# Exchanging the partition halves of odd heads' tokens in a DeltaNet and Fourier-mixing kernel, with other queues for the first loads

## The chip, the core and the metric

The kernel runs on one core of a Trainium2 chip. The metric is the device time of one execution in microseconds (us). The profile is of one execution; its times are counted from the start of the span, in us unless ns is written.

## The reference

Two blocks run one after the other on float32 data. The first is a delta-rule recurrence over 768 tokens for 4 batches and 8 heads of 48 numbers:

```python
def _attn_ref(q, k, v, beta):                       # q, k, v: (4, 8, 768, 48)
    k_n = k / (np.linalg.norm(k, axis=-1, keepdims=True) + 1e-06)
    state = zeros((B, H, D, D))
    for t in range(S):
        kt, vt, bt = k_n[:, :, t], v[:, :, t], beta[:, :, t, None]
        y[:, :, t] = einsum('bhd,bhde->bhe', q[:, :, t], state)
        v_old = einsum('bhde,bhd->bhe', state, kt)
        state = state + bt[..., None] * einsum('bhd,bhe->bhde', kt, vt - v_old)
```

The second takes the result as x of shape (4, 768, 384):

```python
    mixed = np.real(fft(fft(x, axis=1), axis=2))
    u = x + mixed
    un = (u - mean(u)) / sqrt(var(u) + 1e-06)       # over the last axis
    return u + maximum(un @ w_ch1, 0) @ w_ch2       # w_ch1: 384 x 1536, w_ch2: 1536 x 384
```

The two weight matrices come as float64 and are turned into float32 on the chip.

## The kernel before

Tokens are worked on in units: unit u is 128 tokens of one batch with all 8 heads, so there are 4 x 6 = 24 units. Within a unit the recurrence is written for two chunks of 64 tokens. A chunk's own triangular system is inverted, so that its new values are a matrix times v less a matrix times the state; then the state is advanced. One chunk is one step of the recurrence, 12 steps per batch, each of which needs the state left by the one before.

A head is 2j + s, with j from 0 to 3 (NJ) and s 0 or 1; s = 1 are the odd heads. Token c*64 + t of a unit lies in partition c*64 + t, so chunk c is partition half c, for every head. Most matmuls of the recurrence use 64 x 64 corners of TensorE's 128 x 128 array: the row half is the partition half of the operands, the column half is the partition half of the output. `mm` (line 477) and `tr` (line 480) issue all of these matmuls, so their instructions have these two lines, and `copy` (lines 486, 488 and 490) nearly all of the evictions from PSUM.

What the program does, in its own terms:

- Units 0 to 5 (batch 0) are rounds 0 (four units) and 1 (two units). Their keys are loaded first (`load`, line 583), turned (`turn`, line 604), multiplied with themselves (`keys`, line 628), and inverted on VectorE (`begin16` line 777, `invert16` line 838). `queries` (line 1902) then loads q and v. `join` (line 885) and `blocks` (line 953) make the chunk's inverse; its masked copies are ScalarE's.
- Batch 0 then runs `ready`, `values0` (line 1064), `chain0` (line 1081) and `outputs0` (line 1138) per unit. `chain0` accumulates the new values in PSUM (`z.bU`), copies them to u (line 1123), multiplies them with the keys into a state that stays in PSUM (`bS`), and copies that (line 1135). Two odd/even pairs of 64 partitions are copied, one instruction per s.
- Batches 1 to 3 come in rounds of three units: `prepare` (line 1911) and `consume` (line 1925), which calls `blocks`, `ahead` (line 1009), `step` (line 1160) twice and `outputs` (line 1226). In `step`, line 1190 subtracts the state's part from u, line 1219 adds to the state, and in `outputs`, line 1254 adds into x. Lines 1190 and 1254 run once per s on 64 partitions, because the values of chunk c lie in one partition half.
- When a batch's recurrence is complete, `mixing` (line 1869) does the Fourier transforms, the normalisation and the two layers of the MLP. Their matmuls use all 128 rows.

Two matmuls stand for others: line 2036 (early) and line 2043 write PSUM that nobody reads. They are put in by `idle` (line 2029) where TensorE would have nothing.

**What sets the order.** Nothing is issued as it is written. Each piece of work is registered with `P.op` (line 60): the engines that may do it with an estimated cost, what it reads and writes, a priority, and a due time. `Plan.schedule` (line 158) then plays the program through in a model with these costs, the DMA's landing times (eight DMAs in flight, line 279), the clock of TensorE and the fetching of its instructions, and `issue` (line 329) writes the instructions of every engine in the order found. Each engine executes its list in that order. Constants at lines 30 to 46, 529, 1829 and 2000 to 2001 set priorities, hold-backs and due times: `IV` and `IV1` (line 1829) are what rounds 0 and 1 get for the early inversion, `MD` (line 529) is the spacing of the due times of batch 0's units, `E0, E1, D1` (line 2001) bound the stretch in which stand-in matmuls may be put in freely.

**Loads.** All loads but two are issued by SyncE (SP) at line 525. A load of a unit's q, k or v is one DMA of 128 partitions x 8 heads x 192 bytes; for units 6 to 13 it is two, of 121 and 7 partitions (`ROW`, line 585). `bt` (beta) and `pack` (identity and masks) are issued by ScalarE. `f_b` (line 1851) turns beta by six small matmuls and `g_b` (line 1860) copies it to `bcol`.

Of the kernel before, what the change touches and what calls it, by code (L numbers as in the profile page):

```python
# [32 lines left out]
LOOK, HOLD, EARLY = 1e9, 0.2, 25.7  # L33
# [3 lines left out]
LATE = 0.0  # L37
# [8 lines left out]
TARGET, SPANW = 692.9, 2.6  # L46


class Plan:
# [108 lines left out]
    def schedule(self, pick, limits, switch, idle=None, span=()):  # L158
# [27 lines left out]
        self.bursts = []  # L186
        done, n, now = 0, len(ops), 0.0
        order, strict, last = [], True, None
        while done < n:
            progressed = False  # L190
            for e in self.ENG:
# [74 lines left out]
                dur = o.engs[e]  # L266
                if e == "PE":
# [111 lines left out]
def kernel(  # L379
# [24 lines left out]
    GS = 6  # L404
# [137 lines left out]
    def unit(u):  # L542
# [10 lines left out]
        z.K = v(512, 512, "p (h t) -> p h t", h=H)  # L553
        z.V = v(1024, DM, "p (h t) -> p h t", h=H)
# [14 lines left out]
        z.Q = z.LT  # L569
# [8 lines left out]
        z.U = z.ut.rearrange("p (h d) -> p h d", h=H)  # L578
# [4 lines left out]
    def load(z, what):  # L583
        pr = 0
        for x0, x1 in ((0, ROW), (ROW, 128)) if 6 <= z.u < 14 else ((0, 128),):
            rows = slice(z.T * 128 + x0, z.T * 128 + x1)
            kb = 200 * (x1 - x0) / 128
            if "k" in what:
                dma(z.K[x0:x1, :, 0:D], k[z.b, :, rows, :].rearrange("h p d -> p h d"),
                    [z.aK(x0, x1)], pr, kb=kb)  # L590
            if "q" in what:
                dma(z.Q[x0:x1, :, 0:D], q[z.b, :, rows, :].rearrange("h p d -> p h d"),
                    [z.aLT(x0, x1)], pr, kb=kb)
            if "v" in what:
                dma(z.V[x0:x1], v[z.b, :, rows, :].rearrange("h p d -> p h d"), [z.aV(x0, x1)], pr,
                    [units[GS - 1].aK()] if z.u < GS else [], kb=kb)
# [7 lines left out]
    def turn(z, pr, what=(1, 0), after=()):  # L604
# [3 lines left out]
        def fn(e):  # L608
            for i, a in enumerate(what):
                w = (z.Q, z.K)[a].rearrange("p (j s) t -> p j (s t)", s=2)  # L610
# [56 lines left out]
    def gram(z, ro, ul, pr):  # L667
# [4 lines left out]
        def fn(e):  # L672
            for j in range(NJ):
                for s, c in ((0, 0), (1, 1), (0, 1), (1, 0)):
# [3 lines left out]
                       z.QK[pr_, 0:n, c, j, :], j == 0)  # L678
# [33 lines left out]
    def scale_v(z, ro, ul, pr):  # L712
        def fn(e):
            I(eng(e).tensor_tensor(  # L714
                z.V, z.V, ro.nr(160 + 8 * ul, 8)[:, :, None].broadcast_to([128, H, D]),
                op=ALU.mult))
        vec(DM, fn, [ro.anr(160, 32)], [z.aV()], pr)
# [167 lines left out]
    def join(z, ul, ro, pr):  # L885
# [17 lines left out]
        for a in range(2):  # L903
            P.op({"ACT": t_act(256) + 0.08}, lambda e, a=a: copy(e, F[:, :, a], Du, (m0, m1)[a]),
# [12 lines left out]
        for a in range(2):  # L917
            P.op({"ACT": t_act(256) + 0.08}, lambda e, a=a: copy(e, F[:, :, a], E, (m0, m1)[a]),
# [90 lines left out]
    def ahead(z, pr):  # L1009
# [3 lines left out]
        def f1(e):  # L1013
            for j in range(NJ):
                for s, c in ((0, 0), (1, 1), (1, 0), (0, 1)):
                    a = slice(64 * c, 64 * c + 64)
                    mm(psum(b1[c])[64 * s:64 * s + 64, 64 * j:64 * j + 64], z.K[a, 2 * j + s, :],
                       z.TT[a, 2 * j + s, :], j == 0)

        def f2(e):  # L1020
            for j in range(NJ):
                for s, c in ((0, 0), (1, 1), (1, 0), (0, 1)):
                    a, x = slice(64 * c, 64 * c + 64), 64 * (c ^ s)
                    mm(psum(b2[s])[x:x + 64, D * j:D * j + D], z.TT[a, 2 * j + s, :],
                       z.V[a, 2 * j + s, :], j == 0)
# [7 lines left out]
        us = z.ut.rearrange("p (j s d) -> p s j d", s=2, d=D)  # L1033
        W = DM // 2

        def g2(e):
            copy(e, us[:, 0], psum(b2[0])[:, 0:W].rearrange("p (j d) -> p j d", d=D))
        P.op(either(W, 0.1), g2, [], [A(z.ut, 0, DM, 0, 1), A(z.ut, 0, DM, 64, 65)], pr - EV,
             use=[b2[0]], lat=LA)
        for c in range(2):  # L1040
            def g3(e, c=c):
                a, x = slice(64 * c, 64 * c + 64), slice(64 - 64 * c, 128 - 64 * c)
                copy(e, us[a, 1], psum(b2[1])[x, 0:W].rearrange("p (j d) -> p j d", d=D))
# [116 lines left out]
    def step(z, c, pr):  # L1160
# [8 lines left out]
        for i in range(k):  # L1169
# [34 lines left out]
            if n == 2 * NT - 1:  # L1204
                continue
# [875 lines left out]
```

## Time and profile before

| | us |
|---|---|
| median of three runs | 671.3 |
| the three runs | 664.39, 671.3, 673.06 |
| the profiled execution | 667.22 |
| its span | 665.4 |
| TensorE busy (PE) | 650.6 |
| VectorE busy (DVE) | 504.1 |
| ScalarE busy (ACT) | 270.3 |
| GpSimd busy (POOL) | 36.3 |
| mean clock granted to TensorE | 0.997 of full speed |

PE is a matmul, PEld a weight load, which may overlap with matmuls. Each matmul of this kernel is two records in the profile, so 16 matmuls are x32. A matmul's shape is written rows*columns of the stationary operand, then the output's shape. In a group's line the numbers after the bar are its busy time in us, the mean duration of one in ns, and the idle time before it with what ended it. In a table by stretches, the columns behind the length are the engines' busy times, then the granted clock, the share of time for which the 16 DMA engines were busy, and GB/s.

### The profile page before, as it was taken

What the parts mean: (1) busy time and instruction counts of PE and PEld (TensorE: products, weight loads), DVE (VectorE), ACT (ScalarE), POOL (GpSimd) and SP (SyncE); (2) the same over time, 40 slices, a digit from 0 to 9 for tenths busy, and PEclk for the clock granted to TensorE, in tenths of its full rate; (3) what the DMA queues carried; (4) which work ended last, traced back from release to release, by engine and by line L of the source; (5) the groups of instructions that cost most, each with busy time, mean ns of one, the idle gap of its engine ahead of it and who ended that gap; (6) DMA issues with size and microseconds to landing.
All of it is one profiled execution on the core that took longest, in us unless ns stands there. A gap on an engine that the chain in (4) does not pass through costs nothing.

```text
span 665.4 us, 23378 instructions
## 1 busy us (share of the span) xinstructions
PE 650.6 (98%) x10184; PEld 535.8 (81%) x10184; DVE 504.1 (76%) x1479; ACT 270.3 (41%) x758; POOL 36.3 (5%) x34
## 2 busy tenths in 40 slices
PE   8998899999899999999999999999999999999998
PEld 7888888777678777877777778777777789999997
DVE  3998589999964399999922589998981865877473
ACT  5579787621354332524333433244324313321220
POOL 3004223130000000000000000000000000000000
PEclk9999899999999999999999999999999999999999
DMA  9905565100033113001212120000000000000000
GB/s 201 304 33 105 146 142 148 35 0 25 1 63 75 38 26 73 1 1 26 63 38 50 50 49 2 24 2 3 26 2 3 26 3 0 25 1 25 1 25 25
DMA packets 82667, 31.38 MB, mean 47 GB/s; under 512 B 75651, under 2 KB 79716, under 8 KB 82436
## 3 DMA queue, kind: packets, MB, share of 16 engines
q1 hardware_dynamic: 82372, 29.65, 18.0%
q8 instruction: 80, 1.31, 0.8%
q10 hardware_dynamic: 192, 0.23, 0.1%
q14 instruction: 23, 0.19, 0.1%
HBM read 25.16 MB, written 4.72 MB: 45 GB/s over the span
## 4 chain that ended last, share of the span: by engine, by line
PE 80%; DVE 13%; ACT 3%; issue 2%; DMA 1%; DVEq 0%; SPq 0%; ACTq 0%
PE pp L477 75%; PE pp L480 3%; DVE rr L938 2%; DVE tmp L933 2%; ACT us L486 1%; PE pp L2043 1%; PE pp L2036 1%; DMA x<-in_moe_w_ch_dram 1%; DVE rr L795 1%; DMA us<-in_q_dram 1%; DVE tmp L855 1%; DVE w L861 1%; DVE us L714 0%; ACT w L1795 0%; DVE us L696 0%
## 5 line engine op out<-in xcount | busy, mean ns | idle before, releaser
L477 PE MATMUL pp<-R,w 128*128 128x256 f32 (+1 forms) x832 | 184.1, 368 | 0.6 <-ACT R L486 0.6
L477 PEld LDWEIGHTS pp<-R,w 128*128 128x128 f32 x832 | 145.1, 190 | 19.7 <-ACT R L486 0.7
L477 PE MATMUL pp<-w,R 128*128 128x384 f32 x384 | 135.1, 495 | 0.0
L477 PEld LDWEIGHTS pp<-w,R 128*128 128x128 f32 x384 | 70.0, 190 | 41.0 <-issue 0.2
L486 ACT ACTIVATE us<-pp 128x256 f32<-128x256 f32 (+3 forms) x186 | 65.0, 388 | 61.6 <-PE pp L477 48.3
L1475 ACT ACTIVATE R<-pp 128x512 f32<-128x512 f32 x48 | 28.7, 597 | 106.8 <-PE pp L477 106.8
L477 PE MATMUL pp<-us 64*64 64x48 f32 (+3 forms) x2496 | 61.7, 235 | 1.6 <-issue 1.3
L938 DVE TENSOR_TENSOR rr<-rr,tmp 128x108 f32<-128x108 f32 (+13 forms) x180 | 57.6, 330 | 2.3
L477 PEld LDWEIGHTS pp<-us 64*64 64x64 f32 (+1 forms) x2496 | 52.3, 136 | 8.7 <-issue 5.5
L933 DVE TENSOR_TENSOR tmp<-rr 128x210 f32<-128x210 f32 (+12 forms) x180 | 57.3, 328 | 2.1
L1190 DVE TENSOR_TENSOR u<-u,pp 64x192 f32<-64x192 f32 x66 | 22.4, 351 | 39.3 <-PE pp L477 37.7
L477 PEld LDWEIGHTS pp<-u,us 64*64 64x64 f32 x1472 | 39.7, 134 | 14.7 <-issue 10.5
L477 PE MATMUL pp<-u,us 64*64 64x48 f32 x1472 | 45.7, 221 | 2.8 <-issue 1.3
L486 ACT ACTIVATE x<-pp 64x192 f32<-64x192 f32 (+1 forms) x81 | 25.2, 324 | 54.2 <-PE pp L477 50.1
L1254 DVE TENSOR_TENSOR x<-x,pp 64x192 f32<-64x192 f32 x66 | 23.2, 351 | 24.5 <-PE pp L477 23.3
L486 ACT ACTIVATE R<-pp 128x192 f32<-128x192 f32 (+7 forms) x80 | 22.5, 333 | 43.0 <-PE pp L477 21.8
L1650 DVE TENSOR_TENSOR us<-us,pp 128x256 f32<-128x256 f32 x64 | 26.7, 418 | 12.5 <-ACT us L486 10.3
L477 PE MATMUL pp<-tab,R 128*96 128x193 f32 (+2 forms) x192 | 33.0, 328 | 0.1
L477 PEld LDWEIGHTS pp<-st,us 48*64 48x64 f32 x1232 | 22.6, 134 | 12.3 <-issue 9.8
L477 PEld LDWEIGHTS pp<-tab,R 128*96 128x96 f32 (+2 forms) x192 | 30.8, 163 | 1.4 <-DVE R L1279 0.6
L2043 PE MATMUL pp<-pack 64*64 64x256 f32 (+1 forms) x206 | 31.1, 384 | 0.0
L486 ACT ACTIVATE u<-pp 64x192 f32<-64x192 f32 (+1 forms) x68 | 22.2, 326 | 17.0 <-PE pp L477 11.7
(165 smaller groups left out, 978.1 us busy)
## 6 DMA issues: line engine op xcount, KB each, us to landing
out_dram<-x SPq DMA_DIRECT2D x11, 384.0 KB
us<-in_k_dram SPq DMA_DIRECT2D x16, 192.0 KB
us<-in_q_dram SPq DMA_DIRECT2D x16, 192.0 KB
us<-in_v_dram SPq DMA_DIRECT2D x16, 192.0 KB
us<-in_v_dram SPq DMA_DIRECT2D x8, 181.5 KB
ws<-in_moe_w_ch_dram SPq DMA_DIRECT2D x3, 484.0 KB
us<-in_k_dram SPq DMA_DIRECT2D x8, 181.5 KB
us<-in_q_dram SPq DMA_DIRECT2D x8, 181.5 KB
```

Source lines behind the costliest of these rows:

```text
L477: I(nc.tensor.matmul(o, lhsT=lhsT, rhs=rhs, start=start, stop=stop, skip_group_check=True))
L480: I(nc.tensor.matmul(o, lhsT=src, rhs=ident[p0:p0 + n, p0:p0 + n], is_transpose=True, start=start, stop=True, skip_group_check=True))
L486: I(nc.scalar.activation(o, i, ACT.Copy, **({} if scale is None else {"scale": scale})))
L795: vec(1760, lambda e: I(nc.vector.transpose(R, ro.gd(0, 4).rearrange("p (n c) -> p c n", c=32))), [ro.agd(0, 4)], [aR], pr)
L855: I(eng(e).tensor_tensor(T_, sub(j + 1, 16, j, j + 1).broadcast_to([128, 2, n, j]), sub(j, j + 1, 0, j).broadcast_to([128, 2, n, j]), op=A ...
L933: I(eng(e).tensor_tensor(T_, R[:, :, j + 1:32, j:j + 1].broadcast_to([128, ns, n, j]), R[:, :, j:j + 1, 0:j].broadcast_to([128, ns, n, j]) ...
L938: I(eng(e).tensor_tensor(R[:, :, j + 1:32, 0:j], R[:, :, j + 1:32, 0:j], T_, op=ALU.add))
L1190: I(nc.vector.tensor_tensor(U[:, s], U[:, s], psum(b1[s])[a, s0:s1].rearrange("p (j d) -> p j d", d=D), op=ALU.subtract))
L1254: I(nc.vector.tensor_tensor(w, w, v, op=ALU.add))
L1475: I(nc.scalar.activation(o, s, ACT.Relu))
L1650: vec(256, lambda e: I(nc.vector.tensor_tensor(o, i0(), i1(), op=ALU.add)), [], [aH] + list(wr), pr - EV, use=n)
L2043: I(nc.tensor.matmul(pst[two[0]][x, 0:256], lhsT=w[x, 0:n], rhs=w[x, 0:256], start=True, stop=True, skip_group_check=True))
```

## The change

For odd heads, k and v (and q from unit 6 on) are loaded with their partition halves exchanged: tokens 64 to 127 into partitions 0 to 63 and the reverse. Chunk c of head 2j + s is then partition half c ^ s. The new values of one chunk fill all 128 partitions, even heads in one half and odd heads in the other, and u is stored chunk by chunk (c, j, d). The row and column halves of the matmuls, their banks and the copies follow from that. Beta is needed in both arrangements. A load is three DMAs: the even heads, and the odd heads in two halves; for units 0 to 5, keys and values may go to SP or to ScalarE, and the queries are loaded as before the exchange in one DMA. `SPLIT` no longer cuts `step` (it was 1 there). Many constants of the planner are different, some estimated costs too, so all engines' lists are made anew. The core of the diff:

```diff
-LOOK, HOLD, EARLY = 1e9, 0.2, 25.7
+LOOK, HOLD, EARLY = 1e9, 0.181, 25.7
-GAP2 = 0.304
-PLOOK, PHOLD, PEND = 23.4, 0.367, 116.9
+GAP2 = 0.885
+PLOOK, PHOLD, PEND = 15.4, 0.154, 91.9
-FORCE = 540.9
-BLOCK, LEAD, SEEK, LAND, HOLDUP = 256, 60, 1.0, 2.4, 0.0
+FORCE = 548.4
+BLOCK, LEAD, SEEK, LAND, HOLDUP = 256, 60, 1.0, 2.4, 0.4
+CHARGE = 0.9
-TARGET, SPANW = 692.9, 2.6
+TARGET, SPANW = 709.5, 2.6
...
+                if e == "POOL" and o.port:
+                    self.lock = now + 0.2
+                if e == "DVE" and not o.banks and self.lock < now < free["POOL"]:
+                    self.lock, dur = 1e9, dur + CHARGE
...
     def dma(o, i, wr, pr, rd=(), kb=200, q="SP"):
-            I((nc.sync if q == "SP" else nc.scalar).dma_start(out=o, in_=i))
-        P.op({q: 0.45}, fn, rd, wr, pr, lat=2.0, kb=kb)
-    M0, MP, MX, MN, MA, MT, MD = 91.8, 128.0, 19.9, 38, 17.7, 5.85, 4.52
+            I(eng(e).dma_start(out=o, in_=i))
+        t = 0.45 if kb > 100 else 0.6
+        P.op({"SP": t, "ACT": 0.46} if q == "ANY" else {q: t}, fn, rd, wr, pr, lat=2.0, kb=kb)
+    M0, MP, MX, MN, MA, MT, MD = 99.6, 128.0, 22, 39.1, 12.7, 5.85, 6.22
...
     def load(z, what):
-        for x0, x1 in ((0, ROW), (ROW, 128)) if 6 <= z.u < 14 else ((0, 128),):
...
+            if y == "q" and z.u < GS:
+                dma(t[:, :, :, 0:D].rearrange("p s j d -> p j s d"),
+                    w[z.b, :, r0:r0 + 128, :].rearrange("h p d -> p h d"), [wr()], pr, rd)
+                continue
+            for s, x0, x1, o in ((0, 0, 128, 0), (1, 0, 64, 64), (1, 64, 128, -64)):
+                dma(t[x0:x1, s, :, 0:D],
+                    w[z.b, s:H:2, r0 + x0 + o:r0 + x1 + o, :].rearrange("h p d -> p h d"),
+                    [...], pr, rd, kb=100 * (x1 - x0) / 128,
+                    q="ANY" if z.u < GS else "SP")
...
     def ahead(z, pr):          # the evictions of the values
-            copy(e, us[:, 0], psum(b2[0])[:, 0:W]...)            # 128 partitions
-        for c in range(2):
-                copy(e, us[a, 1], psum(b2[1])[x, 0:W]...)        # 64 partitions
+        for s in range(2):
+            for c in range(2):
+                    a, x = slice(64 * c, 64 * c + 64), 64 * (c ^ s)
+                    copy(e, z.ut[a, W * (c ^ s):W * (c ^ s) + W], psum(b2[s])[x:x + 64, 0:W])
...
     def values0(z, pr):
-                        a, y = slice(64 * c, 64 * c + 64), 64 * (c ^ s)
-                        mm(psum(z.bU[s])[y:y + 64, D * j:D * j + D], z.TT[a, 2 * j + s, :], z.V[a, 2 * j + s, :], j == 0)
+                        a = slice(64 * (c ^ s), 64 * (c ^ s) + 64)
+                        mm(psum(z.bU[c])[a, D * j:D * j + D], z.TT[a, 2 * j + s, :], z.V[a, s, j, :], j == 0)
...
     def chain0(z, c, pr, part=(0, 1)):
-        for s in range(2):
-                copy(e, z.ut.rearrange("p (j s d) -> p s j d", s=2, d=D)[a, s],
-                     psum(z.bU[s])[y:y + 64, 0:W].rearrange("p (j d) -> p j d", d=D))
+        P.op(either(W, 0.02), lambda e: copy(e, z.ut[:, W * c:W * c + W], psum(z.bU[c])[:, 0:W]),
+             [], aU, pr - EV - 5, use=[z.bU[c]], lat=LA)
...
     def outputs0(z, pr):
-                        a = slice(64 * c, 64 * c + 64)
-                        mm(psum(z.bO[s])[a, ...], z.LT[a, 2 * j + s, :], z.U[a, 2 * j + s, :], ...)
+                        a = slice(64 * (c ^ s), 64 * (c ^ s) + 64)
+                        mm(psum(z.bO[s])[64 * c:64 * c + 64, ...], z.LT[a, 2 * j + s, :], z.U[a, c, j, :], ...)
...
     def step(z, c, pr):
-                            for q, y in ((1, 64 * c), (0, 64 - 64 * c)):
-                                mm(psum(b1[s])[y:y + 64, D * j:D * j + D], z.QK[r, q, c, j, :], so[r, D * j:D * j + D], j == js[0])
+                        for q, y in ((1, half_(s)), (0, half_(1 - s))):
+                            mm(psum(b1[1 - q])[y, D * j:D * j + D], z.QK[r, q, c ^ s, j, :], so[r, D * j:D * j + D], j == 0)
-                [z.aQT(), z.aE(1, c), A(so, s0, s1)]
+                [z.aQT(), z.aE(1, 0), z.aE(1, 1), A(so, 0, W)]
-                for s in range(2):
-                        I(nc.vector.tensor_tensor(U[:, s], U[:, s], psum(b1[s])[a, s0:s1]..., op=ALU.subtract))
+                I(nc.vector.tensor_tensor(U, U, psum(b1[0])[:, 0:W], op=ALU.subtract))
-                        mm(t[64 * s:64 * s + 64, ...], z.K[a, 2 * j + s, :], z.U[a, 2 * j + s, :], j == js[0])
+                    mm(t[64 * s:64 * s + 64, ...], z.K[half_(s), s, j, :], z.U[half_(s), c, j, :], j == 0)
...
     def outputs(z, pr):
-                    a, y = slice(64 * c, 64 * c + 64), 64 * (c ^ s)
-                    mm(psum(b[c])[y:y + 64, ...], z.LT[a, h, :], z.U[a, h, :], j == 0)
+                    a = slice(64 * (c ^ s), 64 * (c ^ s) + 64)
+                    mm(psum(b[s])[64 * c:64 * c + 64, ...], z.LT[a, h, :], z.U[a, c, j, :], j == 0)
-        for c in range(2):
-            for s in range(2):
+        for s in range(2):
+            for cs in ((0,), (1,)) if z.T == 0 else ((0, 1),):
...
-    NW, IV, IV1, WP = 8, 18.9, 9.07, -14.4
+    NW, IV, IV1, WP = 8, 7.32, 9.07, -8.86
...
+        for T in range(NT):        # in f_b: beta with its halves exchanged
+            for c in range(2):
+                x = 128 * T + 64 - 64 * c
+                mm(t[64 * c:64 * c + 64, ...], bt[:, x:x + 64], ident[0:B * H, 0:B * H], False)
...
-    WAIT, GATHER, URGENT, FIRST = 6.3, 1.59, 8.45, 15
-    E0, E1, D1 = 1.0, 10.0, 125.6
+    WAIT, GATHER, URGENT, FIRST = 14.4, 1.47, 9.13, 14.2
+    F0, F1 = 255.0, 275.0
+    E0, E1, D1 = 0.502, 10.0, 117.8
...
-    P.schedule(pick, LIM, SW, idle, ((E0, D1),))
+    P.schedule(pick, LIM, SW, idle, ((E0, D1), (F0, F1)))
```

Where a line of the diff was long, "..." stands for the part that both sides share.

More of the change, by code (lines that the diff above doesn't have):

```diff
@@ new lines, in step, with f2, g2 @@
+        if n == 2 * NT - 1:
+            return
+        b2 = Bank("attn")
+        def f2(e):
+            t = psum(b2)
+            for j in range(NJ):
+                for s in range(2):
+                    mm(t[64 * s:64 * s + 64, D * j:D * j + D], z.K[half_(s), s, j, :],
+                       z.U[half_(s), c, j, :], j == 0)
+        def g2(e):
+            if n == 0:
+                copy(e, sn[:, 0:W], psum(b2)[:, 0:W])
+            else:
+                I(nc.vector.tensor_tensor(sn[:, 0:W], so[:, 0:W], psum(b2)[:, 0:W], op=ALU.add))
@@ L1226, in outputs @@
+        P.op({"PE": 0.4}, f2, [z.aK(), aU], [], pr, "64", new=b2, lat=LE, col=144, ni=32)
+        vec(W + 30, g2, [A(so, 0, W)] if n else [], [A(sn, 0, W)], pr - EV - 5, use=[b2])
     def outputs(z, pr):
```

212 lines of the change are left out of this document (86 added, 126 removed).

## The prediction

> **What bounds the kernel now.** I read the totals first, then busy time by stretch, then TensorE's stand-in matmuls (lines 2036 and 2043, whose products nobody reads) in the same stretches, then the timeline of one step of the recurrence of batch 0, then the groups that the edit touches.
>
> ```profile
> span 665.4 us, 23378 instructions
> PE 650.6 (98%) x10184; PEld 535.8 (81%) x10184; DVE 504.1 (76%) x1479; ACT 270.3 (41%) x758; POOL 36.3 (5%) x34
> ```
>
> TensorE is busy for 98% of the span. The question is how much of that is work. The stretches, all instructions (columns: length, then PE, PEld, DVE, ACT, POOL busy):
>
> ```profile
> 0.00:40.00 40.00, 36.77 (x744) 32.09 (x744) 29.19 (x116) 21.97 (x62) 5.78 (x10) 1.00 0.83 220
> 40.00:100.00 60.00, 55.37 (x1940) 50.21 (x1936) 47.69 (x110) 51.75 (x142) 16.89 (x14) 0.97 0.49 112
> 100.00:187.00 87.00, 84.38 (x851) 64.40 (x850) 84.88 (x245) 36.54 (x104) 12.73 (x8) 1.00 0.15 40
> 187.00:665.40 478.40, 474.12 (x6662) 389.07 (x6662) 342.36 (x1011) 160.01 (x453) 0.94 (x3) 1.00 0.11 26
> ```
>
> and line 2043 alone (PE, PEld):
>
> ```profile
> 0.00:40.00 40.00, 19.39 (x152) 14.11 (x152) 1.00 0.83 220
> 40.00:100.00 60.00, 6.70 (x38) 2.57 (x38) 0.97 0.49 112
> 187.00:665.40 478.40, 4.34 (x14) 2.23 (x14) 1.00 0.11 26
> ```
>
> So after 187 us TensorE is idle for 478.40 - 474.12 = 4.3 us and in stand-ins for 4.3: 470 of 478 us are work, and nothing that shortens another engine there is worth more than those 8.6 us. Before 40 us it is the other way round: 3.2 idle, 19.4 in line 2043 and 5.4 in line 2036. From 40 to 100 it idles 4.6 and stands in for 6.7. Time can be won only where TensorE does no work, and nearly all of that lies before 100 us.
>
> The recurrence of batch 0, its first part, on ScalarE and then on TensorE:
>
> ```profile
> 48.77 0.66 ACT L486 ACTIVATE u<-pp 64x192 f32<-64x192 f32 x2
> ...
> 51.96 0.67 ACT L486 ACTIVATE u<-pp 64x192 f32<-64x192 f32 x2
> ```
>
> ```profile
> 51.99 0.67 PE L477 MATMUL pp<-us 64*64 64x48 f32 x29
> 52.59 0.50 PE L477 MATMUL pp<-us,pb 64*32 64x32 f32 x18
> 53.79 0.43 PE L477 MATMUL pp<-us,pb 64*32 64x32 f32 x14 [0.70 <-issue]
> 54.15 0.49 PE L477 MATMUL pp<-u,us 64*64 64x48 f32 x10
> ...
> 57.36 1.50 PE L477 MATMUL pp<-u,us 64*64 64x48 f32 x45
> ```
>
> Two u copies run one after the other on ScalarE before the state's matmuls (54.15) may start; TensorE serves other units meanwhile. "issue" is a stop with nothing to wait for in the record.
>
> The groups that shrink:
>
> ```profile
> L1254 DVE TENSOR_TENSOR x<-x,pp 64x192 f32<-64x192 f32 x66 | 23.2, 351 | 24.5 <-PE pp L477 23.3 <-ACT pb L486 0.2
> L1190 DVE TENSOR_TENSOR u<-u,pp 64x192 f32<-64x192 f32 x66 | 22.4, 351 | 39.3 <-PE pp L477 37.7 <-ACT x L486 0.4
> L486 ACT ACTIVATE u<-pp 64x192 f32<-64x192 f32 x47 | 15.2, 324 | 2.3 <-PE pp L477 0.8 <-DVE u L488 0.5
> L1219 DVE TENSOR_TENSOR st<-st,pp 128x192 f32<-128x192 f32 x30 | 10.5, 350 | 12.4 <-PE pp L477 12.0
> ```
>
> 192 columns cost 350 ns on 64 partitions (line 1190) and on 128 (line 1219): joining two halves saves a whole instruction.
>
> **The change part by part**, against the profiled execution: 667.22 us, a span of 665.4 and 1.8 around it. The three runs took 664.39, 671.3 and 673.06; it lies 0.6% below their median.
>
> *Tiles of TensorE.* Each matmul is two records; in starts of the trace, a group that uses all four 64x64 corners starts a matmul every 29 ns (the step's first group, 32 records, from 339.43 to 339.93: 0.50 us), one that uses two corners every 58 ns (the step's second group, 16 records at 343.30 in about 0.46). The change permutes corners. In `step` the first group keeps four and the second two; `ahead` keeps its corners; `outputs` keeps four. In batch 0, `values0` falls from four to two: 0.60 us (51.99 to 52.59) to 0.93. `outputs0` rises from two to four: the 45 records at 57.36 are it and a state group, 1.29 - 0.46 = 0.83, to 0.50. Six units: +2.0 and -2.0. Sum 0.
>
> *Recurrence of batch 0.* The two u copies become one on 128 partitions: 12 steps by 0.33 = 3.9 us of ScalarE and of latency. In the six even steps it goes off the path, 2.0 us. In the odd ones `values0` of the next unit lies between the two matmul groups, as at 51.99; it now ends 0.93 - 0.60 = 0.33 later and itself takes the copies' place: 5 of them win nothing. So 2.0 to 2.3. Is it TensorE's too? From 50 to 100 us it does no work for 8.3 us (4.1 idle, 4.1 of stand-ins), 3.5 of that being four "issue" stops that a shorter copy does not touch. 4.8 are left, so 2.0 can be taken up if other work is not what the next group stands behind; the steps are 4.8 us apart (state copies from 50.65 to 98.54, ten intervals), though their parts add up to 2.7, so mostly it is. Bounds 0 and -3.9; I take -1.2, between them and nearer 0, as the row of 4.8 says.
>
> *Steps, ahead and outputs of batches 1 to 3.* 33 subtractions of 0.351 fewer (11.6 us of DVE), 30 additions fewer (10.5), 18 copies of 0.324 more. All lie after 187 us beside TensorE at 99%; DVE waits there for PE (37.7 and 23.3 us), not the reverse. The step's first group now waits for both evictions of `ahead`, at most 0.4 us later per unit; MLP matmuls queue beside it. Bounds -1.5 (the few idle us at 187 and 277) and +0.4; I take -0.3. Without that cover the saving would be 0.35 a step, 11 us.
>
> *Loads.* Batch 0: keys and values 3 DMAs for 1, on SP or ACT by turns; later units 9 per unit for 6 (units 6 to 13) or 3: 84 more issues on SP, at some 0.3 to 0.6 us each, beside an SP that does little else. The bytes are the same, in 192-byte packets that fill the engines (0.89 to 1.04 of DMA share in the first 30 us): the six key loads run back to back from 2.3 to 8.2 us. A second issuer finds no idle DMA engines. Against the change: ACT issues at 0.41 to 0.48 us; nine key DMAs there are 4 us before its first copy at 6.99, where it has waited 4.0. In the trace each issue takes one of eight semaphores in turn, so a DMA is held back until the eighth before it has landed, and the pieces are smaller now. Keys late by x move the start of the front by x, under which TensorE has only stand-ins. Bounds -0.5 and +2.0; I take +0.5. Values (9 issues on ACT, 4 us) fall where ACT idles about 8 us, before 35 us. Queries stay one DMA.
>
> *Instruction fetch.* TensorE's "issue" stops between 50 and 80 us (0.70, 0.54, 0.92, 1.30) all fall within streams of 192-byte packets. The loads of units 6 to 13 were cut 121 + 7 rows and are now 64 or 128. Later units already load 128 rows, from 192 us on, with no stop over 0.25 us. Bounds: 0, and a stop of the mean 0.86 at each of the 16 fetches between 40 and 105 us, 13.8 less the 3.5 there are: +10.3. I take +0.7, one more, nearer the row after 192 us.
>
> *Beta.* 12 more small matmuls at about 0.06 and a second copy of 0.25 at 7 us, under stand-ins and a DVE that waits 4.3: 0.
>
> *Order.* Tuning numbers change, so every queue is dealt anew. After 187 us there are about 65 round trips between 128-row and 64-row matmuls, each dearer by about 0.1 going in and 0.1 coming out (a first start-to-start of 427 for 322 ns, 320 for 216): 13 us, of which a tenth either way is 1.3. The front can shift by several us. I can show no sign: 0, within ±5. One half-speed window (the clock is 0.91 and 0.92 in the two slices around 80 us) costs 1.7 and may come or go.
>
> Sum: -1.2 - 0.3 + 0.5 + 0.7 = -0.3: 666.9 us.
>
> **Rivals.** *The new order shortens the front.* Round 0's inversion on DVE (20.42 to 35.2) is interleaved with others: after 26.59 round 1's lines 821 and 828 (0.75, 0.68), three of line 696 (1.26) and one of line 714 (0.54), 3.2 together; before it, round 1's line 795, of which about 1.6 stand in the way. ScalarE then makes 13 masked copies of 0.51 for four units before the first u copy; unit 0 needs four: 4.6. Nothing in the edit does this, but the order may. All of it: -9.4, 657.5 against the profiled time. For: TensorE has only stand-ins under it. Against: round 1 and those units are then due later.
>
> *The front gets longer.* The same lever the other way, with late keys: 3 us to 20 (round 1's chain, some 13.5 us of DVE, wholly ahead, keys 2.0 late, all the masked copies), about 677; a third of it, with a fetch stop or a half-speed window more, passes 2%. For: priorities of the inversion fall from 18.9 to 7.32 in round 0. Against: due times, which spread by 6.22 for 4.52 a unit, still put it first.
>
> *Fetch stops at every load* (the slower side by one mechanism): +10.3, 677. It passes 2% when 16 stops grow from 0.86 to about 1.3. The Trainium skill, DMA: Bandwidth & Descriptors, section Why a DMA increments its semaphore by 16 and not by 1, has the engine count as the largest divisor up to 16: 11 of the engines for 121 rows, all 16 for 64 or 128. By that rule the old cut left engines free and the new one does not; the rows after 192 us do not bear out a cost.
>
> *Two row halves in one bank.* `step` and `outputs` now write a bank from both halves of the array. If such writes took turns, four corners would go at two corners' pace: 33 x 0.47 + 18 x 0.47 + 2.0 = +26, 693. Against: `values0` of before writes each bank from both halves and takes 0.60 us for 16. The Trainium skill, TensorEngine Tiling (Array Packing), Gotcha 1, says that row tiles cannot access one bank at the same time; the row at 51.99 does not show that as lost time.
>
> **How the numbers follow.** Little moves, 0.46; front shorter 0.20; front longer 0.19; fetch stops 0.10; one bank 0.05. The time is that of the first, 667, with 662 to 673 its own range. The whole range goes from 656 (the shorter front, with 1.5 from the steps) to 682 (the longer front but for its last 5 us, and most of the fetch stops). 2% of the median, 13.4 us, is about what a measurement of this kernel can tell from no change: below 658 or above 685. Faster: rather more than half of the shorter front, 0.12. Slower: one bank 0.05, four tenths of the fetch stops 0.04, a third of the longer front 0.06: 0.15. Within: 0.73.
>
> **What would show it.** Right: the u copies of batch 0 are 12 or so of 128x192; the DVE lines of 1190 and 1254 fall to 33 and 36 instructions at 350 ns; `values0` takes 0.93 and `outputs0` 0.50; TensorE's idle plus stand-ins stay near 48 us; the state copies still end within 3 us of 99. Wrong: a first u copy before 45 or after 53 us; "issue" stops over 7 us before 105; half-speed windows in number; `step`'s first group at 0.9 us; or TensorE idle after 187 us over 10 us.

## The result and the profile after

The changed kernel takes 674.01 us (median of 22 runs, 669.02 to 681.67), the kernel before 668.84 in its 22 runs beside them: ratio 1.0071, 95% interval 1.0044 to 1.0099. It is slower by 0.7%; the forecast was 667, no change. The profiled execution took 673.43 us with a span of 671.3, 5.9 more than the span of before, at a mean granted clock of 0.987 for 0.997.

The totals of the changed kernel, then its busy time by stretch (columns as before: length, PE, PEld, DVE, ACT, POOL, clock, DMA share, GB/s), then the groups that shrank:

```profile
span 671.3 us, 23577 instructions
PE 655.3 (98%) x10206; PEld 535.8 (80%) x10206; DVE 486.7 (73%) x1420; ACT 271.2 (40%) x761; POOL 34.0 (5%) x34
```

```profile
0.00:40.00 40.00, 35.03 (x594) 26.27 (x596) 24.72 (x98) 18.65 (x52) 5.78 (x10) 0.91 0.84 209
40.00:100.00 60.00, 54.57 (x1959) 49.44 (x1956) 45.99 (x106) 49.47 (x134) 17.11 (x13) 0.99 0.47 109
100.00:187.00 87.00, 85.75 (x765) 66.31 (x764) 78.05 (x225) 34.37 (x99) 10.20 (x8) 0.95 0.18 47
187.00:671.30 484.30, 479.95 (x6895) 393.82 (x6893) 337.95 (x994) 168.76 (x476) 0.93 (x3) 1.00 0.11 26
```

```profile
L1184 DVE TENSOR_TENSOR u<-u,pp 128x192 f32<-128x192 f32 x33 | 11.6, 352 | 35.0 <-PE pp L482 27.8 <-ACT R L1459 5.9 <-ACT pb L491 0.7
L1238 DVE TENSOR_TENSOR x<-x,pp 128x192 f32<-128x192 f32 x30 | 9.3, 351 | 19.9 <-PE pp L482 13.0 <-ACT R L1459 4.0 <-ACT us L1666 2.7
```

The edit does what it says: 33 subtractions where there were 66, at 352 ns on 128 partitions, and VectorE is busy 17 us less. None of that is where the time went. I cut both executions at three events: the first copy of u (batch 0's recurrence begins), the last copy of u, and the first subtraction of a step of unit 6 (line 1190, now 1184).

| us | before | after | difference |
|---|---|---|---|
| up to the first u copy | 48.77 | 54.22 | +5.45 |
| recurrence of batch 0 | 51.56 | 49.62 | -1.94 |
| from there to the first subtraction | 91.76 | 96.03 | +4.27 |
| the rest | 473.35 | 471.41 | -1.94 |

The two parts that the edit meant are 3.9 us shorter; the other two, at the front and behind the recurrence, are 9.7 us longer. A second profile of the same changed kernel (`e0_after` below) has 54.36, 49.62, 92.62 and 471.80 us: the later front repeats, most of the longer third part does not. From 122.6 to 129.4 us the clock granted to TensorE was 0.5 in the first profile and 1.0 in the second. The same stretch in both, the first profile first:

```profile
122.00:130.00 8.00, 7.95 (x36) 6.22 (x35) 5.95 (x19) 4.55 (x13) 1.33 (x1) 0.57 0.03 9
```

```profile
122.00:130.00 8.00, 7.94 (x51) 6.23 (x52) 7.79 (x23) 5.43 (x15) 1.32 (x1) 1.00 0.05 16
```

Half of these 6.8 us is 3.4, so most of the +4.27 goes with the clock. The later front is told by the chain of waits of the changed kernel ahead of TensorE's longest idle time, 3.79 us up to 31.95 (start, length, what; SPq and ACTq are DMA issues):

```profile
22.61 0.59 SPq L530
23.20 0.04 issue
23.25 0.60 SPq L530
23.85 0.04 issue
23.89 0.43 SPq L530
24.32 0.04 issue
24.37 4.77 DMA us<-in_v_dram
29.16 0.61 ACTq L530
29.77 0.04 issue
29.81 0.63 ACTq L530
30.44 0.05 issue
30.48 0.27 ACT nr L811
30.77 0.32 ACT nr L813
31.10 0.55 ACT w L1779
31.64 0.27 ACT us L491
31.91 0.04 issue
31.95 0.68 PE pp L485 x7
```

Read it from the end. TensorE's transposes (line 485) wait for a ScalarE copy. That copy stands in ScalarE's list behind a small step of round 1's inversion (lines 811, 813) and a weight conversion (line 1779), and these behind two DMA issues of values that they do not need. The issue at 29.16 had waited for the semaphore of an earlier value load to come free, and that load had been issued by SP at the end of a row of issues, most of them 0.6 us long. VectorE waits for line 813 too (2.88 us).

The DMA share by ten microseconds, before, and after:

```profile
0.00:10.00 10.00, 8.82 (x105) 8.08 (x106) 3.20 (x33) 4.26 (x9) 5.78 (x10) 1.00 0.89 179
10.00:20.00 10.00, 8.96 (x251) 7.82 (x249) 6.54 (x10) 8.97 (x28) 0.00 (x0) 1.00 0.95 219
20.00:30.00 10.00, 9.69 (x215) 7.57 (x212) 9.45 (x41) 5.21 (x18) 0.00 (x0) 1.00 1.04 302
```

```profile
0.00:10.00 10.00, 8.82 (x106) 7.89 (x106) 3.26 (x34) 2.36 (x5) 5.78 (x10) 1.00 0.76 146
10.00:20.00 10.00, 10.00 (x268) 7.36 (x266) 6.44 (x13) 9.35 (x26) 0.00 (x0) 1.00 0.77 146
20.00:30.00 10.00, 8.16 (x87) 5.23 (x83) 7.56 (x26) 1.87 (x6) 0.00 (x0) 1.00 0.83 193
```

The DMA engines were nearly full before; now, on the mean of each ten microseconds, a sixth to a quarter of their time is unused although loads are late (last column: 146, 146 and 193 GB/s for 179, 219 and 302). They fill up again only in the hole itself: 0.98 to 1.13 in the half microseconds from 28 to 31.

### The profile page after: what moved, and what is told of

Same layout as the page of the kernel before. It is cut to its first block, busy times and chain, and to the rows that moved or that the text cites. A ratio compares the mean times of both kernels' runs of the same rounds, so it can differ in the third digit from the quotient of the medians.

```text
span 671.3 us, 23577 instructions
## 1 busy us (share of the span) xinstructions
PE 655.3 (98%) x10206; PEld 535.8 (80%) x10206; DVE 486.7 (73%) x1420; ACT 271.2 (40%) x761; POOL 34.0 (5%) x34
## 4 chain that ended last, share of the span: by engine, by line
PE 93%; SPq 3%; issue 1%; DMA 1%; DVE 1%; ACT 1%; ACTq 0%; DVEq 0%
PE pp L482 87%; PE pp L485 3%; SPq L530 3%; PE pp L2036 2%; DMA us<-in_v_dram 1%; DMA us<-in_k_dram 0%; DVE w L1798 0%; ACTq L530 0%; DVE x L1375 0%; DVE mv L1377 0%; ACT us L491 0%; ACT ws L1785 0%; ACT ss L491 0%; ACT w L1779 0%; DVE eo L1368 0%
## 5 line engine op out<-in xcount | busy, mean ns | idle before, releaser
L482 PE MATMUL pp<-us 64*64 64x64 f32 (+3 forms) x2496 | 63.6, 235 | 1.1 <-issue 1.1
L942 DVE TENSOR_TENSOR tmp<-rr 128x30 f32<-128x30 f32 (+9 forms) x180 | 59.4, 333 | 3.2
L947 DVE TENSOR_TENSOR rr<-rr,tmp 128x168 f32<-128x168 f32 (+9 forms) x180 | 58.6, 329 | 3.2
L482 PEld LDWEIGHTS pp<-us 64*64 64x64 f32 (+1 forms) x2496 | 54.7, 135 | 7.6 <-issue 5.2
L482 PEld LDWEIGHTS pp<-u,us 64*64 64x64 f32 x1472 | 36.8, 135 | 14.9 <-issue 11.7
L491 ACT ACTIVATE x<-pp 64x192 f32<-64x192 f32 (+1 forms) x84 | 26.6, 324 | 47.6 <-PE pp L482 45.4
L482 PE MATMUL pp<-u,us 64*64 64x48 f32 x1472 | 42.5, 222 | 1.8 <-issue 1.8
L491 ACT ACTIVATE R<-pp 128x192 f32<-128x192 f32 (+5 forms) x76 | 21.5, 337 | 40.8 <-PE pp L482 24.8
L1184 DVE TENSOR_TENSOR u<-u,pp 128x192 f32<-128x192 f32 x33 | 11.6, 352 | 35.0 <-PE pp L482 27.8
L1634 DVE TENSOR_TENSOR us<-us,pp 128x256 f32<-128x256 f32 x64 | 26.7, 419 | 12.5 <-ACT us L491 10.3
L482 PE MATMUL pp<-st,us 48*64 48x48 f32 x1232 | 27.5, 222 | 1.5 <-issue 1.1
```

The source lines that it names most:

```text
L482: I(nc.tensor.matmul(o, lhsT=lhsT, rhs=rhs, start=start, stop=stop, skip_group_check=True))
L491: I(nc.scalar.activation(o, i, ACT.Copy, **({} if scale is None else {"scale": scale})))
L942: I(eng(e).tensor_tensor(T_, R[:, :, j + 1:32, j:j + 1].broadcast_to([128, ns, n, j]), R[:, :, j:j + 1, 0:j].broadcast_to([128, ns, n, j]) ...
L947: I(eng(e).tensor_tensor(R[:, :, j + 1:32, 0:j], R[:, :, j + 1:32, 0:j], T_, op=ALU.add))
L1184: I(nc.vector.tensor_tensor(U, U, psum(b1[0])[:, 0:W], op=ALU.subtract))
L1634: vec(256, lambda e: I(nc.vector.tensor_tensor(o, i0(), i1(), op=ALU.add)), [], [aH] + list(wr), pr - EV, use=n)
```

## The experiments

Each ratio is to runs of the kernel before on the same chip; the groups of experiments ran on four chips. "First u" is the first u copy of the profiled execution; before has it at 48.77. The expectations name theories by letters and state each.

**The changed kernel again, and its loads on other queues.** First came the suspicion that ScalarE's waiting issues are the cause. `e0_after` is the changed kernel as it is; the next two only change the engine that issues, at the same places of the order; the third lets the planner make the order anew.

```diff
-            I(eng(e).dma_start(out=o, in_=i))
+            I(eng(by or e).dma_start(out=o, in_=i))    # e1: by="SP" for batch 0's values; e2: keys too
-                    q="ANY" if z.u < GS else "SP")
+                    q="SP")                             # e3, order made anew
```

> The changed kernel itself, as the yardstick beside the others. Every theory expects a ratio of 1.004 to 1.010 to the kernel before, a first u copy of batch 0 near 54 us (48.8 before), and a mean clock near 0.987 (0.997 before).

> The values of batch 0 are all issued by SP, at the same places of the planned order; the lists of PE, DVE and POOL are the same, ACT only loses its value DMAs. Theory A (a DMA issue that waits for its semaphore holds up ScalarE, whose evictions TensorE and VectorE wait for): ScalarE's 4.6 us of waits for values and its 4.4 us stop before the square root are gone, TensorE's 3.8 us hole at 28 us too, the first u copy moves from 54.2 to 49 to 51 us, one or two half-speed windows fewer, some 3 to 6 us less time than the changed kernel, ratio about 1.000. Theory B (the new order itself makes the front late, whoever issues): nothing moves, first u copy after 53 us, ratio about 1.007. Theory C (the same descriptors come later in smaller pieces, whoever issues): values land as late on SP, the hole moves but stays, ratio 1.005 to 1.008.

> As the one before, and the keys of batch 0 by SP too, at the same places of the order. Theory A: ScalarE's 7.3 us wait at the keys goes and its table load comes early, but the first turn still waits for the keys; 18 key issues at about 0.6 us on one queue take 11 us, so the last keys land 1 to 3 us later than with two queues: ratio 0.2 to 0.5% above the run with values alone on SP. Theory C: no worse than with two queues, since the DMA engines set the pace. Theory B: ratio about 1.007 as before.

> Keys and values of batch 0 by SP alone, and the plan is made anew with that, so all orders differ. Theory A: ScalarE's list has no DMA issue but pack and beta; no hole over 2 us in TensorE before 40 us; ratio 0.997 to 1.003. Theory B: the new constants still give a late front, first u copy after 53 us, ratio 1.005 or more.

Measured: e0 1.0101 (1.0065 to 1.0138), first u 54.36. e1 1.0125 (1.0084 to 1.0165), first u 57.73. e2 1.0166 (1.0123 to 1.0208), 57.16. e3 1.0387 (1.0345 to 1.043), 60.40. Theory A falls: with no value issued by ScalarE the front is later, not earlier. The chain of e1 shows why:

```profile
24.03 0.61 SPq L530
24.64 0.04 issue
24.69 4.55 DMA ws<-in_moe_w_ch_dram
29.23 0.02 issue
29.26 0.66 ACT w L1779
29.92 0.27 ACT us L491
30.18 0.04 issue
30.23 0.46 PE pp L485 x7
```

The same copy and the same transposes wait, now behind a weight conversion (line 1779) whose block of weights stood in SP's list behind twelve pieces of values. One in-order wait has taken the other's place.

**How many DMAs, and in which kernel.** Now the number of issues alone, in both directions. `f1_whole0` keeps the changed order; `f2` and `f3` keep the order of before. `e4_old_const` asks whether the new order is to blame. Where a load is whole or the odd heads come in one piece (f1, g1 to g3, and units 6 to 13 in h3, i1 and i2), the exchange is left out for it: the work is the same, the values are others.

```diff
     # f1, in the changed kernel: k and v of units 0 to 5 in one DMA at the place of the first piece
-                I(eng(e).dma_start(out=o, in_=i))
+                if (z.u, y) not in done:
+                    I(eng(e).dma_start(out=t[:, :, :, 0:D]..., in_=w[z.b, :, r0:r0 + 128, :]...))
     # f2, f3, in the kernel before: k and v of units 0 to 5
+                for n, (x0, x1, s) in enumerate(((0, 128, 0), (0, 64, 1), (64, 128, 1))):
+                    I(nc.sync.dma_start(out=o[x0:x1, s:H:2], in_=i[x0:x1, s:H:2]))   # f3: SP and ACT by turns
     # e4, in the changed kernel: the constants of before
-GAP2 = 0.885
+GAP2 = 0.304      # and PLOOK, FORCE, HOLDUP, CHARGE, TARGET, M0 to MD, IV, WP, WAIT to FIRST, E0 to F1
```

> The changed kernel with its own order of all engines, but the keys and values of units 0 to 5 come in one DMA each (12 issues for 36), at the place of the first piece and in natural halves; odd heads of batch 0 are therefore not exchanged and batch 0's values are others, the work being the same. Theory C (the pieces: 24 issues more, eight DMAs in flight, make batch 0's loads late): the first u copy comes at 48 to 51 us instead of 54.2, TensorE's hole near 28 us is under 1 us, and the ratio to the kernel before falls from 1.0101 to 1.004 or less. Theory P (the new order sets the front, whatever the loads do): the u copy stays at 53 to 55 us and the ratio at 1.007 to 1.012.

> The changed kernel with the planner's constants of the kernel before; loads and exchange as changed, order made anew from these. Theory C: the pieces are still there, so the front is late still: first u copy after 52 us, ratio 1.005 or more. Theory P: with the old constants the front comes back to within 2 us of 48.8 and the ratio to 1.000 +- 0.004.

> The kernel before, order untouched; only the keys and values of units 0 to 5 are cut in three DMAs each as in the change (even heads, odd heads in two halves), not exchanged, all on SP. Theory C: 24 issues more on SP, of about 0.6 us, make the last values some 8 us later and the first u copy 3 to 9 us later than 48.8; ratio 1.006 to 1.02. Theory P: 48.8 +- 1 and ratio 1.000 +- 0.003.

> As the run before, but half of the pieces (9 of the keys', 9 of the values') are issued by ScalarE, at the same places of the order, as the change does. Theory C: between the kernel before and the cut on SP alone: first u copy 50 to 54.5, ratio 1.003 to 1.010, that is, about the whole of the change's loss without its exchange. Theory P: 48.8 +- 1 and ratio 1.000 +- 0.003.

Measured: f1 0.9992 (0.9954 to 1.003), first u 48.58. f2 1.0123 (1.006 to 1.0187), 55.43. f3 1.0128 (1.0087 to 1.0168), 54.98. e4 1.0199 (1.0136 to 1.0262), 53.04. Theory C stands both ways: taking the pieces out of the changed kernel brings its front back to 48.6, putting them into the kernel before costs 1.2%, beside 0.7 to 1.0% for the whole change. Theory P falls: with the old constants the front is late all the same (53.04), and the time is worse than e0's by about 1%. A second issuer (f3) was expected to lie between the kernel before and f2, and won nothing over SP alone. The same place in f1:

```profile
25.73 0.27 ACT nr L820
26.02 0.32 ACT nr L822
26.34 0.58 ACT w L1788
26.92 0.27 ACT us L491
27.23 0.46 PE pp L485 x7
```

The same instructions run 4.7 us earlier with no DMA in the chain. f1's DMA share in the first three tens is 0.93, 0.91 and 1.05. (Five of its six value loads are SP's, since the first piece stood there.)

**Keys or values, pieces or halves, a third issuer.**

```diff
     # g1: only the values whole (keys cut); g2: only the keys whole; g3: even heads, odd heads, 128 rows each
+                    if z.u < GS and y == "v" else None)
     # g4: the change complete, the 64-row pieces of batch 0's values from GpSimd
+                    by="POOL" if z.u < GS and y == "v" and s else None)
```

> The changed kernel with its own order; only the keys of units 0 to 5 are cut in three (18 issues), their values are one whole DMA each (6 issues for 18) in natural halves, so that odd heads of batch 0 get other values. Theory K (late keys move the start of the front and all behind it): most of the 5.6 us between the whole loads and the change is here, first u copy 52 to 54.5, ratio 1.006 to 1.011. Theory V (the values' issues, queued at 14 to 30 us on SP and ACT, are what is late): first u copy 48.5 to 50.5, ratio 1.003 or less. If the two add, each gives 2 to 4 us.

> The counterpart: values of units 0 to 5 cut in three, keys whole in natural halves (so that batch 0's odd heads get other keys). Theory K: first u copy 48.5 to 50.5, ratio 1.003 or less. Theory V: 52 to 54.5, ratio 1.006 to 1.011, with TensorE's hole near 28 us and ACT's wait for the values' DMA.

> The changed kernel with its own order; keys and values of units 0 to 5 in two DMAs each, even heads and odd heads, of 128 rows both (24 issues for 36; odd heads of batch 0 in natural halves, so its values are others). By number of issues (theory C) it lies between one piece (first u copy 48.6, 0.999) and three (54.3, 1.010): 50 to 52.5 us and 1.002 to 1.007. If it is the 64 rows of a piece that are slow, it is as good as one piece: 48.5 to 49.5 and at most 1.002.

> The changed kernel complete, with the twelve 64-row pieces of the odd heads' values (units 0 to 5) issued by GpSimd, which has nothing to do from 6 to 52 us, at the same places of the order; SP and ACT have 12 issues fewer. Theory C in the form that the issues of SP and ACT and their common eight semaphores are short: last values earlier, first u copy 49.5 to 52.5, ratio 1.000 to 1.006. Rival: small DMAs are slow whoever issues them, or GpSimd's issues cost more than 1 us each: first u copy 53.5 or later, ratio 1.008 or more.

Measured: g1 0.9976 (0.9931 to 1.0021), g2 1.0046 (1.0004 to 1.0088), g3 1.0004 (0.9965 to 1.0043), g4 1.0024 (0.9984 to 1.0064). The first u copy of g1, g2 and g4:

```profile
50.12 0.33 ACT L491 ACTIVATE u<-pp 128x192 f32<-128x192 f32 x1 [0.22 <-PE pp L482]
```

```profile
54.80 0.33 ACT L491 ACTIVATE u<-pp 128x192 f32<-128x192 f32 x1 [0.22 <-PE pp L482]
```

```profile
50.47 0.33 ACT L491 ACTIVATE u<-pp 128x192 f32<-128x192 f32 x1 [0.22 <-PE pp L482]
```

It is the values (theory V): cut keys cost 1.5 us of front, cut values 6.2, both together 5.8 (e0 less f1). g2's ratio is lower than expected for V. Two pieces cost 1.4 us (49.96), the third, which also halves the rows, four more. In g4 the twelve issues of GpSimd run from 6.25 to 14.1 us at 0.62 to 0.76 us each, on eight semaphores of their own, and the front is back within 1.7 us with the exchange whole.

**The hole, and the rest.** Open then: whether TensorE's hole at 28 us and the half-speed stretch behind it make the loss, and where the 2 us won in the recurrence go when the front is in time.

```diff
     # h1, in the changed kernel: the last stand-ins before the hole nine times
+            for _ in range(9 if n == 198 else 1):
     # h2: all 18 value pieces by GpSimd
     # h3 = g4, and units 6 to 13 in natural halves, rows 0:121 and 121:128 (2 DMAs for 3)
     # h4 = g4, and units 6 to 13 cut once more: 121 + 7, and 55 + 9 twice (6 DMAs for 3)
     # i1 = the change with the loads of h3 for units 6 to 13, batch 0 untouched
     # i2 = g4, and units 6 to 13 in one DMA of 128 rows, natural halves
```

> The changed kernel with eight more pairs of stand-in matmuls on TensorE just ahead of the transposes that wait at 28 us (3.7 us of work, as long as the hole); loads untouched, the front is as late as in the change. Theory H (the hole takes the clock down, and the lower mean clock is most of the loss): the half-speed window at 30 to 37 us is gone, the mean clock over the runs rises from 0.985-0.987 to 0.990 or more, ratio 1.001 to 1.006. Rival (the lateness of the front is the loss, the clock follows from other places): clock and ratio stay at 0.984 to 0.988 and 1.007 to 1.012.

> The changed kernel complete, all 18 pieces of the values of units 0 to 5 issued by GpSimd (12 in the run before this), so that SP has only keys, queries and weights. If the weights' place behind the values on SP still costs: first u copy 49 to 50.3 against 50.47, ratio 0.997 to 1.002. If the limit is the 16 DMA engines' share by then: first u copy 50.3 to 52, ratio 1.001 to 1.006.

> The changed kernel with 12 value pieces issued by GpSimd, and q, k and v of units 6 to 13 loaded as before the change: all heads in natural halves, as 121 and 7 rows (2 DMAs for 3, batch 1's and part of batch 2's odd heads are not exchanged, so their values are others). Theory F (what the joined copies won in the recurrence of batch 0 is lost to stops of TensorE's issue while these loads run, since the pieces of 128 and 64 rows occupy all 16 DMA engines): stops between 50 and 110 us fall from 6.4 to 3 to 4.5 us, the last copy of u comes 1.5 to 3.5 us earlier than 99.4, ratio 0.994 to 1.000. Rival (stops come by chance, or by place): 5 us or more, ratio 1.000 to 1.004.

> The changed kernel complete (exchange everywhere), 12 value pieces by GpSimd, and the pieces of units 6 to 13 cut in rows once more: 121 and 7 of the even heads, 55 and 9 of each odd half (6 DMAs for 3). Theory F: stops between 50 and 110 us 3 to 5 us, ratio 0.994 to 1.002, unless the 72 issues more on SP (0.6 us each, 43 us between 50 and 150) make these loads late, which would show as waits of TensorE or VectorE for DMA behind 100 us and a ratio over 1.004.

> The changed kernel, batch 0's loads as in the change (36 pieces on SP and ACT), and only q, k and v of units 6 to 13 loaded as 121 and 7 rows in natural halves (their odd heads are not exchanged, so the values of batch 1 and a part of batch 2 are others). If the two places add: 1.0085 less the 0.0094 between the two runs with batch 0's values on GpSimd: ratio 0.996 to 1.003, with the first u copy at 54.3 still. Rival (the later loads matter only once the front is in time): ratio 1.005 to 1.011.

> As the run with 12 value pieces by GpSimd and 121 and 7 rows for units 6 to 13 (0.993), but these loads are one DMA of 128 rows each (natural halves, same remark on values). If it is the number and size of the DMAs (fewer in a queue of eight, no waiting issue): ratio 0.990 to 0.997. If it is that 121 rows leave DMA engines free: ratio 0.999 to 1.005, with more and longer issue stops than 6.4 us between 50 and 110.

Measured: h1 1.0129 (1.0081 to 1.0176), h2 1.0014 (0.9972 to 1.0056), h3 0.993 (0.989 to 0.997), h4 1.0138 (1.0105 to 1.0172), i1 1.0032 (0.9998 to 1.0067), i2 0.9986 (0.9951 to 1.0021).

Theory H falls: with the hole filled the half-speed stretch at 30 is gone, but the first u copy is as late as in the change (54.23), so the clock there is not what makes the front late. Other half-speed stretches came at 79, 89 and 127, the mean clock of the runs was 0.983, and the time is no better. h2 brought the front to 50.93, no earlier than twelve pieces did. Theory F falls in its mechanism though its time nearly came out (0.993 where 0.994 to 1.000 was expected): the issue stops between 50 and 110 us are 6.4 us in g4, h3 and i2 alike, so loads of 121 and 7 rows did not change them, and h3's last u copy came at 102.45, later than g4's 99.41 and not earlier. One thing that did change is a wait. Of the changed kernel, of h3 and of h4, from 50 to 130 us (who waited for whom: total, times, longest):

```profile
ACT w L1779 <- DMA ws<-in_moe_w_ch_dram: 2.7, 2, 2.0
...
PE pp L485 <- ACT ss L491: 1.2, 1, 1.2
```

```profile
ACT w L1785 <- DMA ws<-in_moe_w_ch_dram: 0.5, 1, 0.5
...
ACT w L1785 <- DMA x<-in_moe_w_ch_dram: 0.4, 1, 0.4
```

```profile
ACT w L1785 <- DMA ws<-in_moe_w_ch_dram: 7.1, 3, 4.8
...
PE pp L485 <- ACT ss L491: 4.0, 1, 4.0
```

It is the front's mechanism again: weights stand in SP's list behind the pieces of the units' loads, ScalarE waits for them in order, and a copy (ss) that TensorE needs for batch 0's transform stands behind. TensorE's wait there is 0 in h3, i1 and i2 (2 DMAs or 1), 0 to 3.1 us in the eleven executions of the changed order with three pieces there (1.2 in the change, 0.4 in e0), and 4.0 in h4 (6).

The stretch from the last u copy to the first subtraction is 92.0, 91.4 and 91.8 us in h3, i1 and i2, from 92.3 to 101.0 in the eleven, and 100.0 in h4. Most of that spread is the clock. There is no half-speed time in it in h3, i1 and i2, nor in e0, g1, g3 and g4, which have three pieces and take 92.3 to 93.1; the other seven (95.6 to 101.0) have 6.8 to 13.6 us of it, and h4 10.2. At full clock three DMAs thus cost about 1 us more there than two or one, and the six of h4, with half of 10.2 taken off, about 3. The ratios of the runs show that the later loads have a price. These profiles explain at most about 1 us of it by the wait; whether more loads also bring the half-speed stretches is not shown, since the same kernel had one here in one profile and none in the other. i2 does not tell the number of DMAs from their rows: its interval reaches into h3's.

The two places add, as far as intervals of 0.3 to 0.4% either way can tell:

| ratio to before | units 6 to 13 in three DMAs | as before the change |
|---|---|---|
| batch 0's values as changed | 1.0071 and 1.0101 | 1.0032 |
| 12 of their pieces by GpSimd | 1.0024 | 0.993 |

From the upper row to the lower 0.5 to 1.0% goes, the price of batch 0's loads; from the left column to the right 0.4 to 0.9%, that of the later ones. What the new instructions and their order win with loads about as cheap as before is 0.7% (h3), some 4.7 us of 669; the loads of the change cost about twice that.

No version that keeps the exchange everywhere is faster than the kernel before: g4 takes back the loss and no more.

## Why the prediction was wrong

- **Recurrence of batch 0, -1.2 (0 to -3.9).** Inside its bounds and of the forecast sign: -1.94. One profile does not carry the size, though: over the 15 executions with the changed order the part takes 48.4 to 57.8 us, and in seven it is longer than the 51.56 before. Most of that is again the clock. The part holds 3.4 us at half speed in the kernel before and none in e0, f1, g1 and g4, which take 48.4 to 49.6; with half of the 3.4 taken off before, the gain is 0.2 to 1.5, the forecast or less.
- **Steps, ahead and outputs, -0.3 (-1.5 to +0.4).** Too small, and outside its lower bound: -1.94. The rest took 470.4 to 471.8 us in every execution with the changed order but h1 (472.7), for 473.3. How much of it is the joined instructions and how much the order is not separated. With the old constants (e4) it was 480.8, and with the new ones but planned anew (e3) 481.2: a new plan alone can move it by 10 us.
- **Tiles of TensorE, 0.** Borne out: `values0` of unit 0 takes 0.97 us (from 53.05, its 32 records in two stretches) for 0.93 forecast (`outputs0` is not timed here), and nothing behind 187 us slowed down, so "two row halves in one bank" is out.
- **Loads, +0.5 (-0.5 to +2.0).** This is the step that failed. It allowed at most 2.0 us, and the front alone is 5.45 later (5.59 in e0, and 0.19 earlier in f1, where batch 0's loads are whole); behind the recurrence another 0.9 (e0) to 4.3, the larger figure mostly with the clock. It had the right rows: "each issue takes one of eight semaphores in turn, so a DMA is held back until the eighth before it has landed, and the pieces are smaller now". It then priced only late keys. Of the values it said that they "fall where ACT idles about 8 us, before 35 us": the busy share counted, not what is queued behind a waiting issue, which is what the chain at 29.16 shows. Of the later loads it said "beside an SP that does little else"; but SP also carries the weights, in order, and ScalarE waits for these in order. And "a second issuer finds no idle DMA engines" was read from the full engines of before; with pieces of a third they were no longer full (0.76 for 0.89). The page that the prediction used has a rule on this that it left aside: the Trainium skill, DMA: Bandwidth & Descriptors, section Rules for kernel authors, says of two transfers to disjoint partition halves "Use one 128-partition transfer". The runs agree with the advice: three pieces for one cost 1.2% in a kernel with nothing else changed (f2), and in the changed kernel two pieces of 128 rows cost 1.4 us of front (g3), three with the odd heads cut in halves 5.8 (e0).
- **Instruction fetch, +0.7 (0 to +10.3).** Inside its bounds: the issue stops between 50 and 110 us are 5.4 us for 3.5, +1.9 (6.7 in e0). The reason given falls: they do not follow the rows of the loads (6.4 with 121 + 7, with 128 and with 128/64/64).
- **Order and clock.** "One half-speed window costs 1.7 and may come or go": there are three stretches at half speed in the changed kernel, at 30.4, 98.7 and 122.6, 17.1 us together for 3.4 before. Half of that, at most 8.5 us, is lost for 1.7; this is no further term, since it lies inside the differences of the four parts. On e0's chip the mean clock of the runs was 0.986 (e0) for 0.993, their mean spans 673.3 and 667.7, and a line through the runs of either gives 5.2 or 4.7 us for 0.01 of clock; at full clock the lines are 1.7 us apart. So by these lines two thirds of the difference goes with the clock. With batch 0's loads whole (f1) the mean clock is 0.994, no lower than that of the kernel before beside it, so the cut loads lower it; in which way is not settled: h1 excludes the hole at 28 us alone.
- **The cases.** "Little moves" had 0.46; "the front gets longer" (0.19, 3 to 20 us, about 677) is what came, by values and not by keys or the order. The text named the sign itself: a first u copy after 53 us. Another of its signs, half-speed windows in number, came too, and the last state copy starts at 102.44, more than 3 us behind 99. TensorE's idle time plus stand-ins is 55.6 us, where "near 48" was forecast; before it was 52.4, since the 48 leaves out the stretch from 100 to 187 us. The whole range, 656 to 682, held the time, and the likeliest case's own range, 662 to 673, missed it by one.

## What to carry to other kernels

Cutting a load into pieces is not free when the bytes stay the same: count the issues, give each the time that an issue of the trace has, and look at what stands behind them in the same queue, other data above all. A wait on an in-order engine is priced by the work queued behind it and by who waits for that work, not by the engine's idle time. When a change both saves instructions and cuts loads, undo the loads alone first: that one run here gave the whole front back. And before a difference is divided among stretches of the span, profile the same kernel twice: here that took most of one stretch's loss off the loads and put it down to the clock.

## What the runs showed of the hardware that was not expected

- A DMA issue takes as long for a piece as for the whole: where it does not wait, about 0.60 us for 64 rows of 4 heads, 0.37 to 0.61 for 128 rows of 4 heads (0.51 for most of g3's and g4's on SP), 0.43 to 0.57 for 128 rows of 8 heads. On SP alone the 18 key pieces (f2) come 0.65 us apart, which for 64 KB on average is about 100 GB/s; the first ten microseconds moved 103 GB/s at a DMA share of 0.56 where whole loads moved 179 at 0.89.
- GpSimd issued 64-row loads at the same pace (0.62 to 0.76 us) with eight semaphores of its own, so that these loads were not held back by SP's and ScalarE's.
